# Hash attention and an MLP mixer on one core: a bounce moved into the token stage, a fourth place for its results, and the order of its weight sums

## The chip, the cores and the metric

The kernel runs on one core of a Trainium2 chip. The metric is the device time of one execution in microseconds, and lower is better. TensorE (PE) multiplies matrices into PSUM, VectorE (DVE) and ScalarE (ACT) do elementwise work, GpSimd (POOL) does a little elementwise work and issues the DMAs that add into their destination, and SyncE (SP) issues nearly all other DMAs. Each engine works through its own instructions in program order, and each waits on semaphores of the others.

## The reference

```python
# attention: B=4, H=8, S=768, D=64, hash buckets of 6 bits
q_bits, k_bits = (q @ proj > 0), (k @ proj > 0)
mask = bucket(q_bits)[..., :, None] == bucket(k_bits)[..., None, :]
attn = softmax(where(mask, q @ k.T / sqrt(D), -1e9))
x = (attn @ v).transpose(0, 2, 1, 3).reshape(4, 768, 512)
# mixer: d_tok=256, d_ch=1536, d_model=512
h = relu(x^T @ w_tok1) @ w_tok2
u = x + h^T
out = u + relu(u @ w_ch1) @ w_ch2
```

## The kernel before

Three stages follow each other: `attention`, `tokens`, `channels`. `XT` holds x transposed (features on the partitions) and stays in SBUF all the time. Attention works on 16 pairs of heads, numbered n = 4·batch + pair; 14 of them run in the loop (`NREG` is 14), the last two by a sorted path.

The token stage needs x with rows on the partitions. So each batch is "bounced": `bounce(stage, n)` turns two pairs of `XT` block by block into a staging tile (two DVE transposes, L233) and stores it with four SP DMAs of 192 KB (L238) to a DRAM tile `bounced[b]`; `fetch(b, x)` loads the batch from there (one SP DMA of 1536 KB, L245). Batch 2 is made of bounces 8 and 10, batch 3 of bounce 12 and the sorted pairs. Bounce 10 is `bounce_late`: it runs in the last pair of the attention stage, at the point "newton". Bounce 12 runs at the start of `tokens`.

`tokens` first allocates `x1`, issues `fetch(1, x1)`, starts the conversion of the second channel weight (`Conversion`, three `raw` buffers, 768 KB each by SP at L169; one piece is an ACT pass at L177 and five DVE operations at L187 to L206), and bounces pair 12. Its loop then goes, in program order:

```python
for b in range(B):
    mix1(b)              # PE L1226, x times W1; relu on ACT, L1233; a job per half
    if b == 0:
        weight_sums()    # W2sums, DVE L1203 to L1206
    left_sums(b)         # DVE L1249 to L1252
    if b:
        mix2(b - 1, 0); job(); mix2(b - 1, 1)
mix2(B - 1, 0); inputs(0, T, 0); mix2(B - 1, 1)
```

x of the batches alternates between `x0` and `x1`; `mix1(b)` ends with the fetch of batch b + 2. `mix2(b, m)` is seven products (PE L1266) in four PSUM banks of eight, four ACT copies (L1271 to L1278), five DVE additions (L1281 to L1285), and one POOL DMA of 768 KB that adds the result into `XT` (L1286). The result stands in one of three places, `places[(2b + m + 1) % 3]`, the thirds of `SW2`. The loop has eleven slots for jobs: two in each `mix1`, one between the two `mix2` of each batch but the last. The jobs are the sums of the first channel weight (one job of four DVE operations, L1316 to L1321) and eight pieces of conversion.

`channels` begins with six blocks `hidden(0, t)` of seven products each (PE L1353). In a block ACT copies three products (p1, p5, p7, L1359), DVE adds p1 and a product into `r[0]` (L1393), ACT copies the united product u, and DVE makes `r[3]`, `r[1]`, `r[2]` from it (L1402); POOL adds p5 to p7 (L1397). Sums of weights on DVE (L1858 to L1861, L1316 to L1321) stand between these, one job inside a block and one behind it. In the program order of ACT the copy of u of one block stands ahead of the copy of p1 of the next, and u is copied after the L1393 of its block.

The token stage's own tiles `W1` (6 KB per partition), `W2` (6 KB) and `x0` (12 KB) are laid one behind the other, at 0, 6 and 12 KB from the place where the pool starts. When that pool is closed, the tiles of `channels` are laid over the same bytes in the order of their allocation: `TB` (8 KB) at 0, `R0` (12 KB) at 8, `R1` (12 KB) at 20, and so on. A tile's first writer waits for the last user of the tiles that lay there. `r[0]` of block t is two rows of 1 KB in `R0`, at t KB and at 6 + t KB from its start. The bytes of `x1` belonged to the bit rows and the exponentials (`exps`) of the attention stage, which its last products (PE L470) read.

Of the kernel before, what the change touches and what calls it, by code (L numbers as in the profile page):

```python
# [36 lines left out]
F32 = mybir.dt.float32  # L37
BF16 = mybir.dt.bfloat16
U32 = mybir.dt.uint32
# [9 lines left out]
def kernel(  # L49
# [17 lines left out]
    P = 128  # L67
# [66 lines left out]
    NW = 768  # L134
# [93 lines left out]
    def bounce(stage, n):  # L228

        b, hp = pairs[n]  # L230
        stage = stage.rearrange("p (a k i) -> p a k i", k=2, i=32)
        for k in range(2):
            nc.vector.transpose(  # L233
                stage[:, :, k], XT[:, hp + k, S * b : S * b + S].rearrange("p (a i) -> p a i", i=32),
            )
        to = bounced[b].rearrange("(a i) (g c) -> g i a c", i=32, g=4)
        for g in range(4):
            nc.sync.dma_start(  # L238
                out=to[g, :, :, 32 * hp : 32 * hp + 64],
                in_=stage[32 * g : 32 * g + 32].rearrange("p a k i -> p a (k i)"),  # L240
            )
# [16 lines left out]
    def attention(pool, psum, W1, W2, x0):  # L258
# [725 lines left out]
            at(back + 2, "begin", call("store"))  # L984
        at(0, "loads", prepare_sorting)

        def bounce_late():
            raw = pool.tile([P, NW, 2], U32, name="raw", tag="raw", bufs=2)
            bounce(raw.rearrange("p n w -> p (n w)").bitcast(F32), NREG - 4)

        at(NREG - 1, "newton", bounce_late)
        at(NREG - 1, "begin", fetch_turned)
        at(NREG - 2, "last", lambda: fetch(0, x0))

# [190 lines left out]
    def tokens(pool, psum, W1, W2, x0, weights, jobs, T, places):  # L1185

        x1 = pool.tile([P, NR, DM], F32, name="x1", tag="x1", bufs=1)
        R1 = {}
        turned = not jobs
        if not turned:
            fetch(1, x1)
            jobs = jobs(weights(pool))
            bounce(places[2], NREG - 2)
        NQ = DM // 2
        sums = pool.tile([P, 3, HALF], F32, name="W2sums", tag="W2sums", bufs=1)
        b00, b01, b10, b11 = (W2[:, k, HALF * n : HALF * n + HALF] for k in range(2) for n in range(2))  # L1200

        def weight_sums():
            nc.vector.tensor_tensor(sums[:, 0], b01, b00, op=ALU.subtract)  # L1203
            nc.vector.tensor_tensor(sums[:, 1], b11, sums[:, 0], op=ALU.subtract)
            nc.vector.tensor_tensor(b01, b11, b01, op=ALU.subtract)
            nc.vector.tensor_tensor(sums[:, 2], b10, sums[:, 1], op=ALU.subtract)  # L1206

        def job():
            if not turned and jobs:
                jobs.pop(0)()  # L1210

        def bank(name):
            return psum.tile([P, 512], F32, name=name, tag="mm", bufs=4 if turned else 8)

        def banks():
            return psum.tile([P, 2, 512], F32, name="trp", tag="tr", bufs=2)

        def mix1(b):
            x = (x0, x1)[b % 2]
            if b and turned:  # L1220
                turn(b, x, banks)
            r1 = pool.tile([P, NJ, DM], F32, name="r1", tag="r1", bufs=2)
            for j in range(NJ):
                ps = bank("t1")
                for r in range(NR):
                    nc.tensor.matmul(  # L1226
                        ps, W1[:, r, P * j : P * j + P], x[:, r], start=(r == 0), stop=(r == NR - 1),
                    )
                to = r1[:, j]
                if not turned:  # L1230
                    to = to.rearrange("p (c g i) -> p g c i", c=NCB, i=32)
                    ps = ps.rearrange("p (g c i) -> p g c i", c=NCB, i=32)
                nc.scalar.activation(to, ps, ACT.Relu)  # L1233
                job()
            if b % 2:
                new = pool.tile([P, 3, NQ], F32, name="r1s", tag="r1s", bufs=1)
            else:
                new = T[0].rearrange("p k t -> p (k t)")[:, : 3 * NQ].rearrange("p (i c) -> p i c", i=3)
            R1[b] = r1, new
            if not turned and b + 2 < B:  # L1240
                fetch(b + 2, x)

        def left_sums(b):
            r1, new = R1[b]
            a00, a01, a10, a11 = (
                r1[:, k].rearrange("p (m i c) -> p i m c", m=2, i=2)[:, i] for i in range(2) for k in range(2)
            )
            new = new.rearrange("p i (m c) -> p i m c", m=2)
            nc.vector.tensor_tensor(new[:, 1], a00, a10, op=ALU.subtract)  # L1249
            nc.vector.tensor_tensor(a10, a10, a11, op=ALU.add)  # L1250
            nc.vector.tensor_tensor(new[:, 0], a10, a00, op=ALU.subtract)
            nc.vector.tensor_tensor(new[:, 2], a01, new[:, 0], op=ALU.subtract)  # L1252

        def mix2(b, m):

            r1, new = R1[b]
            a00, a01, s1, a11 = (
                r1[:, k, P * (2 * m + i) : P * (2 * m + i) + P] for i in range(2) for k in range(2)
            )
            new = new[:, :, P * m : P * m + P]  # L1260
            ps = [bank("t2")[:, :HALF] for _ in range(4)]
            to = places[(2 * b + m + 1) % 3].rearrange("p (i n t) -> p i n t", i=2, n=2)
            p1, u, p7, p57 = (to[:, i, n] for i in range(2) for n in range(2))

            def product(at, left, right, start=True):
                nc.tensor.matmul(  # L1266
                    ps[at], left, right, start=start, stop=True, skip_group_check=True,
                )

            product(0, a00, b00)  # L1270
            nc.scalar.copy(p1, ps[0])  # L1271
            product(1, a01, b10)
            product(2, s1, sums[:, 0])
            nc.scalar.copy(p57, ps[2])
            product(3, new[:, 1], b01)
            nc.scalar.copy(p7, ps[3])
            product(0, new[:, 0], sums[:, 1], False)
            nc.scalar.copy(u, ps[0])  # L1278
            product(2, new[:, 2], b11, False)
            product(3, a11, sums[:, 2], False)  # L1280
            nc.vector.tensor_tensor(p1, ps[1], p1, op=ALU.add)  # L1281
            nc.vector.tensor_tensor(p57, p7, p57, op=ALU.add)
            nc.vector.tensor_tensor(p57, p57, u, op=ALU.add)
            nc.vector.tensor_tensor(p7, ps[3], u, op=ALU.add)
            nc.vector.tensor_tensor(u, ps[2], u, op=ALU.add)  # L1285
            nc.gpsimd.dma_start(  # L1286
                out=XT[:, 2 * m : 2 * m + 2, S * b : S * b + S], in_=to.rearrange("p i n t -> p i (n t)"),
                accum_op=ALU.add,
            )

        for b in range(B):
            mix1(b)
            if b == 0:
                weight_sums()
            left_sums(b)
            if b:
                mix2(b - 1, 0)
                job()
                mix2(b - 1, 1)
        mix2(B - 1, 0)  # L1300
        inputs(0, T, 0)
        mix2(B - 1, 1)
        while not turned and jobs:
            job()
# [937 lines left out]
    def attention_and_tokens(W1, W2, x0):  # L2242
        inside(attention, W1, W2, x0)
        pool = late.enter_context(tc.tile_pool(name="late", bufs=1, side="right", reuse_waits="tile"))
        SW1 = big["SW1"] = pool.tile([P, 3, NCB // 2, DCH // 2], F32, name="SW1")
        TA = big["TA"] = pool.tile([P, 2, NCB // 2, TT], F32, name="TA")
        n = NHT * DM

        def second_tile(i):
            return pool.tile([P, (n, n * 3 // 4)[i]], F32, name=f"second{i}", tag=f"second{i}", bufs=1)  # L2250

        WC2 = second["WC2"] = second_tile(0).rearrange("p (k c) -> p k c", k=NHT)
        second["SW2"] = second_tile(1).rearrange("p (i k c) -> p i k c", i=3, k=NHT // 2)
        second["tile"] = second_tile

        def weights(pool):
            return Conversion(pool, [(w_ch2, WC2, 3, (0, NHT))], bufs=3)

        def jobs(conversion):
            early, late = weight_sums(  # L2260
                WC1, SW1, slice(0, NCB // 2), slice(NCB // 2, NCB), slice(0, DCH // 2), slice(DCH // 2, DCH),
            )
            return [
                lambda: (early(), late()),
                *[conversion.one] * (NHT * DM // NW),
            ]

        SW2 = second["SW2"].rearrange("p i k c -> p i (k c)")
        places = [SW2[:, i] for i in range(3)]
        inside(tokens, W1, W2, x0, weights, jobs, [TA[:, 0], None, TA[:, 1], None], places)  # L2270
# [100 lines left out]
```

## Time and profile before

| | |
|---|---|
| median of 3 runs | 766.55 us (766.54 to 766.57) |
| the profiled execution | 767.96 us, span 766.2 us |
| busy in the span | PE 758.5, DVE 673.5, ACT 442.4, POOL 189.7 us |
| the token stage begins (first PE L1226) | 289.1 us |
| the channel stage begins (first PE L1353) | 367.6 us |

Times in the trace are microseconds from the span's start. PE stands for the matmuls and PEld for the weight loads ahead of them; an engine followed by q is its sequencer, so SPq lists the DMAs that SP issues. In a row of the timeline stand start, duration, engine, line, operation, output and inputs, the count, and in square brackets how long the engine had been idle and what ended that.

### The profile page before, as it was taken

What the parts mean: (1) busy time and instruction counts of PE and PEld (TensorE: products, weight loads), DVE (VectorE), ACT (ScalarE), POOL (GpSimd) and SP (SyncE); (2) the same over time, 40 slices, a digit from 0 to 9 for tenths busy, and PEclk for the clock granted to TensorE, in tenths of its full rate; (3) what the DMA queues carried; (4) which work ended last, traced back from release to release, by engine and by line L of the source; (5) the groups of instructions that cost most, each with busy time, mean ns of one, the idle gap of its engine ahead of it and who ended that gap; (6) DMA issues with size and microseconds to landing.
All of it is one profiled execution on the core that took longest, in us unless ns stands there. A gap on an engine that the chain in (4) does not pass through costs nothing.

```text
span 766.2 us, 14575 instructions
## 1 busy us (share of the span) xinstructions
PE 758.5 (99%) x5549; PEld 509.8 (67%) x5549; DVE 673.5 (88%) x969; ACT 442.4 (58%) x816; POOL 189.7 (25%) x266
## 2 busy tenths in 40 slices
PE   9999999999999999999999999999999999999997
PEld 4565655666656554455444468888877888886886
DVE  5899899899997998999788798998899799889884
ACT  6677777677776873333232326566666667665331
POOL 2346771638761820011220100100000011000001
PEclk9999999999999999999999999999999999999999
DMA  7746587575965549876697997889576696750665
GB/s 257 271 172 184 179 240 225 181 179 186 217 202 116 168 68 254 310 178 119 112 321 244 348 360 263 244 233 277 171 220 210 234 261 140 235 157 8 207 157 130
DMA packets 131210, 157.80 MB, mean 206 GB/s; under 512 B 56000, under 2 KB 99520, under 8 KB 129216
## 3 DMA queue, kind: packets, MB, share of 16 engines
q1 hardware_dynamic: 119248, 136.05, 56.3%
q0 software_dynamic: 11600, 20.53, 13.1%
q8 instruction: 45, 0.74, 0.4%
q10 hardware_dynamic: 288, 0.25, 0.1%
q14 instruction: 29, 0.24, 0.1%
HBM read 107.71 MB, written 40.67 MB: 194 GB/s over the span
## 4 chain that ended last, share of the span: by engine, by line
PE 88%; DVE 8%; DMA 2%; issue 1%; SPq 0%; DVEq 0%; ACT 0%; ACTq 0%
PE b L1353 51%; PE sc L503 16%; PE acc L470 14%; PE sc L425 1%; PE hash L536 1%; PE ss L848 1%; DVE size L196 1%; PE sacc L874 1%; DVE unit L195 1%; DMA XT<-second 1%; DVE second L206 1%; PE hash L348 1%; DVE size L191 1%; PE ssums L862 1%; PE hash L353 1%
## 5 line engine op out<-in xcount | busy, mean ns | idle before, releaser
L414 ACT ACTIVATE exps<-sc 128x768 f32<-128x768 f32 (+1 forms) x181 | 126.5, 765 | 10.1 <-PE sc L503 7.2
L1353 PE MATMUL b<-R,second 128*128 128x256 f32 (+1 forms) x522 | 131.8, 408 | 0.0
L503 PE MATMUL sc<-qk 32*128 32x384 f32 (+1 forms) x1352 | 120.1, 457 | 0.0
L1353 PEld LDWEIGHTS b<-R,second 128*128 128x128 f32 x522 | 99.1, 190 | 28.5 <-issue 16.5
L470 PE MATMUL acc<-exps,vn 128*32 128x385 f32 (+1 forms) x1344 | 111.7, 486 | 0.0
L503 PEld LDWEIGHTS sc<-qk 32*128 32x128 f32 x1352 | 92.3, 185 | 16.9 <-issue 4.4
L1359 ACT COPY c<-b 128x256 f32<-128x256 f32 (+1 forms) x96 | 40.3, 426 | 79.3 <-PE b L1353 66.1
L470 PEld LDWEIGHTS acc<-exps,vn 128*32 128x32 f32 x1344 | 43.9, 109 | 62.0 <-issue 60.0
L376 POOL DMA_DIRECT2D bits<-XT x104 | 54.6, 526 | 72.1 <-DVE XT L366 27.4
L459 DVE TENSOR_TENSOR esd<-esd,exps 128x768 f32<-128x768 f32 x70 | 67.0, 957 | 4.3
L1353 PE MATMUL b<-XT,WC 128*128 128x256 f32 (+1 forms) x208 | 61.0, 428 | 0.0
L791 POOL DMA_INDIRECT table<-XT,sorting x48 | 57.1, 1190 | 14.7 <-issue 13.2
L2063 POOL DMA_DIRECT2D out<-second x7 | 8.5, 1213 | 187.3 <-DVE second L2057 81.5
L557 ACT COPY rec<-rec 32x384 f32<-32x384 f32 x56 | 28.5, 510 | 41.0 <-DVE rec L551 39.6
L1353 PEld LDWEIGHTS b<-XT,WC 128*128 128x128 f32 x208 | 39.5, 190 | 15.4 <-issue 10.3
L503 PE MATMUL sc<-bits 32*128 32x384 bf16 (+1 forms) x338 | 48.0, 311 | 0.0
L1353 PE MATMUL b<-XT,SW 128*128 128x256 f32 (+1 forms) x164 | 47.0, 410 | 0.0
L455 DVE TENSOR_TENSOR esd<-esd,exps 128x768 f32<-128x768 f32 x42 | 40.3, 958 | 4.4
L1226 PE MATMUL t<-x,W 128*128 128x512 f32 x96 | 42.1, 594 | 0.2 <-DMA x<-bounced 0.2
L1353 PEld LDWEIGHTS b<-XT,SW 128*128 128x128 f32 x164 | 31.1, 190 | 9.4 <-issue 4.1
L1286 POOL DMA_DIRECT2D XT<-second x8 | 9.9, 1233 | 95.8 <-DVE unit L187 56.2
L1226 PEld LDWEIGHTS t<-x,W 128*128 128x128 f32 x96 | 18.1, 190 | 23.3 <-issue 21.7
(333 smaller groups left out, 1455.9 us busy)
## 6 DMA issues: line engine op xcount, KB each, us to landing
second<-left SPq DMA_DIRECT2D x20, 768.0 KB
qk<-in_qk_rows SPq DMA_DIRECT2D x13, 1152.0 KB
raw<-in_moe_w_ch SPq DMA_DIRECT2D x16, 768.0 KB
second<-left SPq DMA_DIRECT2D x18, 576.0 KB
WC<-hidden_left SPq DMA_DIRECT2D x18, 448.0 KB
x<-bounced SPq DMA_DIRECT2D x4, 1536.0 KB
XT<-second POOLq DMA_DIRECT2D x8, 768.0 KB
seen<-in_qk SPq DMA_DIRECT2D x15, 384.0 KB
```

The source lines that it names most:

```text
L376: nc.gpsimd.dma_start(out=to[at : at + 2 * BITS, half[j]], in_=g[of : of + 2 * BITS])
L414: return nc.scalar.activation(e[:, :, columns], sc, ACT.Exp, scale=SCALE)
L455: nc.vector.tensor_tensor(self.d, self.d, e, op=ALU.add)
L459: nc.vector.tensor_tensor(self.d, self.d, e, op=ALU.add)
L470: made = nc.tensor.matmul(acc[D * i + d : D * i + d + 32], vn[:, i, c, d : d + 32], e[:, i], start=(c == 0), stop=(c == NR - 1),)
L503: nc.tensor.matmul(made[j, piece][:, i], k[at : at + 32, ks], q[at : at + 32], start=part < 0, stop=part == 1,)
L557: nc.scalar.copy(rec[other : other + 32, h], rec[at : at + 32, h])
L791: nc.gpsimd.indirect_dma_start(out=tables[2 * w + i], out_offset=bass.IndirectOffsetOnAxis(ap=self.at[:, x : x + 1], axis=0), in_=row, in_ ...
L1226: nc.tensor.matmul(ps, W1[:, r, P * j : P * j + P], x[:, r], start=(r == 0), stop=(r == NR - 1),)
L1286: nc.gpsimd.dma_start(out=XT[:, 2 * m : 2 * m + 2, S * b : S * b + S], in_=to.rearrange("p i n t -> p i (n t)"), accum_op=ALU.add,)
L1353: nc.tensor.matmul(ps, left(k), right(k), start=start and k == ks[0], stop=stop and k == ks[-1], skip_group_check=True,)
L1359: nc.scalar.copy(c, ps)
```

## The change

Four things: bounce 10 leaves the last pair of attention and is issued at the start of `tokens`, behind the fetch of batch 1 and the first two weight pieces, ahead of bounce 12, through `places[1]`. `weight_sums()` is called ahead of the loop. The last `mix2` writes its result into the first 6 KB per partition of `x0` and not into a third of `SW2`. The sums of the channel weight become two jobs (`early`: L1316, L1317; `late`: L1320, L1321), so that there are ten jobs for the eleven slots.

```diff
-        def bounce_late():
-            raw = pool.tile([P, NW, 2], U32, name="raw", tag="raw", bufs=2)
-            bounce(raw.rearrange("p n w -> p (n w)").bitcast(F32), NREG - 4)
-
-        at(NREG - 1, "newton", bounce_late)
         at(NREG - 1, "begin", fetch_turned)
...
             fetch(1, x1)
             jobs = jobs(weights(pool))
+            bounce(places[1], NREG - 4)
             bounce(places[2], NREG - 2)
...
-            to = places[(2 * b + m + 1) % 3].rearrange("p (i n t) -> p i n t", i=2, n=2)
+            place = places[(2 * b + m + 1) % 3]
+            if b + 1 == B and m:
+                place = x0.rearrange("p r c -> p (r c)")[:, : 2 * S]
+            to = place.rearrange("p (i n t) -> p i n t", i=2, n=2)
...
+        weight_sums()
         for b in range(B):
             mix1(b)
-            if b == 0:
-                weight_sums()
             left_sums(b)
...
-                lambda: (early(), late()),
+                early, late,
                 *[conversion.one] * (NHT * DM // NW),
```

## The prediction

> **What bounds the kernel now.** I read the page first, then the list of waits for PE alone, then the timeline engine by engine around the token stage.
>
> ```profile
> PE 758.5 (99%) x5549; PEld 509.8 (67%) x5549; DVE 673.5 (88%) x969; ACT 442.4 (58%) x816; POOL 189.7 (25%) x266
> PE t L1226 <- DMA x<-bounced: 0.2, 1, 0.2
> ```
>
> PE is busy 758.5 of 766.2 us, and of its listed waits (total, times, longest) this one of 0.2 us is the only one in the token and channel stages. So a removed wait is worth only the hole in PE's matmuls beneath it, and a new wait costs what reaches PE. Matmul ends are modelled, so I measure holes by starts. The chain of waits runs through VectorE from 293 to 358, which I take as a warning about VectorE and not as the bound.
>
> ```profile
> 289.12 10.57 PE L1226 MATMUL t<-x,W 128*128 128x512 f32 x24
> 299.90 10.57 PE L1226 MATMUL t<-x,W 128*128 128x512 f32 x24 [0.22 <-DMA x<-bounced]
> 319.60 10.46 PE L1226 MATMUL t<-x,W 128*128 128x512 f32 x24
> 329.90 1.45 PE L1266 MATMUL t<-W,r 128*128 128x384 f32 x4
> 316.76 0.81 PE L1266 MATMUL t<-W,TA 128*128 128x384 f32 x2
> 317.56 0.30 PEld L1266 LDWEIGHTS t<-W2sums,TA 128*128 128x128 f32 x2 [0.61 <-ACT second L1271]
> 318.31 0.81 PE L1266 MATMUL t<-W,TA 128*128 128x384 f32 x2
> 364.71 0.81 PE L1266 MATMUL t<-W,r1s 128*128 128x384 f32 x2
> 365.07 0.48 ACT L1271 COPY second<-t 128x384 f32<-128x384 f32 x1 [2.91 <-DMA XT<-second]
> 366.35 0.81 PE L1266 MATMUL t<-W,r1s 128*128 128x384 f32 x2
> 367.64 3.60 PE L1353 MATMUL b<-XT,WC 128*128 128x512 f32 x8
> ```
>
> An unhindered `mix1` takes 329.90 - 319.60 = 10.30 us. The first took 299.90 - 289.12 = 10.78, because batch 1 had not landed: a hole of 0.48. Four undisturbed matmuls of `mix2` take 367.64 - 366.35 = 1.29. From 316.76 to 318.31 they took 1.55 (hole 0.26), and from 364.71 to 366.35 they took 1.64 (hole 0.35). The last hole is the copy at 365.07, which waited for a place. All that the change can win here is 0.48 + 0.26 + 0.35 = 1.09 us, 0.14%. A difference of 0.2%, 1.53 us, is about what a measurement of this kernel tells from none.
>
> **The change part by part. Attention's end.**
>
> ```profile
> 285.03 2.15 ACT L557 COPY rec<-rec 32x384 f32<-32x384 f32 x4 [3.71 <-DVE rec L551]
> 285.51 1.83 DVE L233 STREAM_TRANSPOSE raw<-XT 128x768 f32<-128x768 f32 x2
> 287.26 0.92 DVE L561 TENSOR_TENSOR XT<-num,rec 128x768 f32<-128x768 f32 x1
> 285.13 4.06 PE L470 MATMUL acc<-exps,vn 128*32 128x384 f32 x48
> 287.37 3.11 SPq L238 DMA_DIRECT2D bounced<-raw  x4
> 290.65 1.12 SPq L245 DMA_DIRECT2D x<-bounced  x1
> ```
>
> The two transposes of bounce 10 leave a hole in VectorE: the next instruction, L561, needs ACT's copies, which end at 287.18. Removing them wins nothing there (0 to 0.1). On SP the four stores go from ahead of the fetch of batch 1. That fetch then waits for the exponentials under `x1`, which PE reads until 285.13 + 4.06 = 289.2, so it goes 1.45 us earlier. It took 299.90 - 290.65 = 9.25 to be of use, so it would be there by 298.4, ahead of PE at 289.12 + 10.30 = 299.4: the hole of 0.48 closes (0 if the load gains nothing).
>
> **The token stage on SP.**
>
> ```profile
> 297.57 6.35 SPq L238 DMA_DIRECT2D bounced<-second  x4
> ```
>
> Four stores took SP 6.35 us beside the loads. Now eight stand in a row, behind the transposes that still begin at 295.70 (below): at worst to 297.57 + 12.7 = 310.3. Behind them on SP wait the fetch of batch 2 and the third weight piece. A fetch of 9.25 lands at 319.5, PE wants it at 319.60 less 0.48 and 0.26: between 0 and 0.7 us of wait, and I take 0, since the first weight pieces now load earlier. Nor does it matter, as the next step shows. `places[1]` is first rewritten by ACT around 311, after those stores.
>
> **The token stage on DVE.**
>
> ```profile
> 295.70 1.84 DVE L233 STREAM_TRANSPOSE second<-XT 128x768 f32<-128x768 f32 x2
> 304.48 0.56 DVE L187 TENSOR_SCALAR unit<-size 128x768 uint32<-128x768 uint32 x1
> 308.47 0.55 DVE L1203 TENSOR_TENSOR W2sums<-W 128x384 f32<-128x384 f32 x1
> 357.60 0.56 DVE L1285 TENSOR_TENSOR second<-t,second 128x384 f32<-128x384 f32 x1
> 361.55 0.56 DVE L1282 TENSOR_TENSOR second<-second 128x384 f32<-128x384 f32 x1 [0.28 <-ACT second L1276]
> 357.94 1.16 PEld L1266 LDWEIGHTS t<-W,r 128*128 128x128 f32 x4
> 359.87 0.51 PEld L1266 LDWEIGHTS t<-W,r1s 128*128 128x128 f32 x2
> ```
>
> From 295.70 on the timeline marks no idle VectorE until 361.55. So 1.84 us of added transposes shift what follows. The split job moves each conversion piece (308.47 - 304.48 = 3.99) one slot later, so between the first `left_sums` and the last conversions VectorE is 3.99 - 1.84 = 2.15 us early. That makes the first six `mix2` safe, and removes the copy's delay at 317 (0.26 won; 0 if the third weight piece lands late). But the eighth piece then fills the slot of the last `mix1` that was empty, and from `left_sums(3)` on VectorE is 1.84 late. The L1285 of `mix2(2, 0)` ends at 358.16 + 1.84 = 360.0. `mix2(3, 0)` takes over that call's PSUM banks: its weight loads came at 357.94 to 359.87, and would now come 0.48 + 0.26 = 0.74 earlier, but its fourth product needs the bank that L1285 frees. PE is there at 360.06 instead of 359.87: what was won is given back, whatever it was. Cost against before 0.2, bounds -0.74 (bank not needed) to 0.2. The fourth place then removes the wait at 365.07: -0.35. `weight_sums` ahead of the loop is needed later than before and costs nothing of its own. PE enters `channels` about 0.2 us earlier.
>
> **The fourth place.** The place is `x0`'s first 6 KB, bytes 12 to 18 KB of the pool. `R0` lies at 8 to 20 KB, and `r[0]` of block 0 writes 8 to 9 and 14 to 15 KB. So its L1393 must wait until the last accumulating DMA has read the place.
>
> ```profile
> 374.71 1.07 ACT L1359 COPY c<-b 128x512 f32<-128x512 f32 x2 [2.79 <-PE b L1353]
> 358.57 1.20 POOL L1286 DMA_DIRECT2D XT<-second  x1 [6.89 <-DVE second L1285]
> 365.30 1.22 POOL L1286 DMA_DIRECT2D XT<-second  x1 [5.53 <-issue]
> 372.05 1.20 POOL L1286 DMA_DIRECT2D XT<-second  x1 [5.53 <-DVE TB L1183]
> 378.80 1.21 POOL L1286 DMA_DIRECT2D XT<-second  x1 [5.55 <-DVE seen L1859]
> 376.48 0.69 DVE L1393 TENSOR_TENSOR R<-b,c 128x512 f32<-128x512 f32 x1 [5.29 <-ACT c L1359]
> 377.21 0.59 ACT L1359 COPY c<-b 128x512 f32<-128x512 f32 x1 [1.43 <-DVE R L1393]
> 386.52 1.88 PE L1353 MATMUL b<-TB,SW 128*128 128x512 f32 x4
> ```
>
> The last four of these DMAs follow each other on POOL by 6.73 to 6.75 us. The first was read out 365.07 - 358.57 = 6.50 after its start (that ended ACT's wait for the place). With L1285 1.84 later, the last starts at 378.80 + 1.84 = 380.64 and is done at 387.14; without the shift at 385.30. L1393 ran at 376.48: a new wait of some 10.7 us on VectorE. Behind L1393 on VectorE wait the block's other sums and the weight sums; ACT's copy of u waits for L1393 (377.21), and behind it in ACT's order stands the next block's p1, without which PE can't overwrite that bank. So: L1393 at 387.15, u at 387.9, p1 at 388.4 to 389.0 (a copy takes 0.59, two in a row 1.07), PE at 389.05 instead of 386.52. PE loses 2.5 us against before. POOL's own queue is 1.84 later, and nothing there is wanted before VectorE comes free.
>
> ```profile
> 302.80 1.76 DVE L1321 TENSOR_TENSOR SW<-WC,SW 128x1536 f32<-128x1536 f32 x1
> 379.20 2.53 DVE L1861 TENSOR_TENSOR seen<-SW,seen 128x384 f32<-128x384 f32 x1
> 389.41 2.71 DVE L1321 TENSOR_TENSOR second<-second,second 128x1536 f32<-128x1536 f32 x1
> 392.04 0.68 DVE L1393 TENSOR_TENSOR R<-b,c 128x512 f32<-128x512 f32 x1
> 398.54 1.88 PE L1353 MATMUL b<-TB,SW 128*128 128x512 f32 x4
> ```
>
> The next L1393 stands 392.04 - 376.48 = 15.56 us of VectorE work later. Two of its instructions were stretched beside POOL's additions: L1861 by 1.97 (2.53 against the 0.56 of an addition of that size, as L1285 above), L1321 by 0.95 (2.71 against 1.76 at 302.80). The first meeting falls away, since VectorE is waiting then. So it comes at 387.15 + 15.56 - 1.97 = 400.7 (399.8 with neither, 402.7 with both), the second block's p1 is ready 1.8 later as above, and PE goes on at 402.55 instead of 398.54: 4.0 lost in all. From there VectorE is 8.7 late and PE 4.0. The banks of a block are wanted only two blocks on, and a p1 copy that is late by the difference still stands ahead of its PE instruction, so I add nothing.
>
> The sum: 4.0 us on PE's path, which from 367.64 to the end has no hole to take it up. The profiled execution, 767.96, stands 1.4 above the median; the difference is added to the median: 766.55 + 4.0 = 770.5.
>
> **The Trainium skill** ("DMA: Bandwidth & Descriptors", section "Anatomy of one DMA — SWDGE (gpsimd) path") fits a DMA issued from GpSimd as about 2.0 us plus its bytes at 436e3 per us, an estimate of 3.8 us for 768 KB. By that the last one would end at 360.4 + 4 x 3.8 = 375.6, ahead of L1393, and the sum would be 766.3. These rows disagree: 6.75 between starts, 6.50 to the end.
>
> **The rivals.** *A: the accumulate lands in time.* It decides at about 382.8: then L1393 is soon enough for both p1 copies. If the last one started when its sums are ready, at some 370, and took 6.50, it would be done at 376.6. Then 766.55 less 0.2 to 1.09, so 765.5 to 766.3, not slower. Against it stand three equal steps of 6.75 on POOL. The skill's fit would lead here too. *B: the wait is real and PE feels half.* VectorE not later at 358, reading done at 385.30, PE late 0.7 and then 1.3 to 2.2: 767.8 to 768.7. *C: it doesn't end there.* VectorE 8.7 late runs into the stores of its one scratch tile, and at the second layer's first sums it is still late: with both meetings and another stall of 2 us, 772.6 to 774.
>
> **How the numbers follow.** Forecast (3.1 to 6.0 lost, that is 769.6 to 772.6) 0.64; B 0.17; C 0.07; A 0.12. The range 767.8 to 772.6 takes in the forecast and B. Slower by over 0.2% needs over 1.53 us: forecast, C, and most of B, 0.86. Within 0.2%: most of A and the edge of B, 0.11. Faster by over 0.2% needs more than the 1.09 that the holes hold: 0.03.
>
> **What would show it.** In the new trace L1393 of the first block is idle some 10 us, ended by the DMA into XT; PE's list of waits gains the ACT copies of L1359 in the second and third block, 2.5 and 1.5 us; four L1286 still stand 6.75 apart, the last near 380.6; the hole at 299 is gone; `mix2(3, 0)` waits for VectorE. I am wrong if the last L1286 starts before 376, or if L1393 stays near 376.5.

## The result

The changed kernel took 771.07 us (median of 4 runs, 770.79 to 771.38), before 766.55: a ratio of 1.0059, 95% interval 1.0042 to 1.0076. It is slower, by 4.5 us where 4.0 were forecast (770.5).

The profiled execution, 770.79 with a span of 769.1 us, shows where. First its list of waits for PE (total, times, longest):

```profile
PE b L1351 <- ACT c L1357: 3.4, 2, 2.0
PE t L1222 <- DVE second L1280: 0.5, 1, 0.5
PE t L1265 <- ACT second L1270: 0.4, 1, 0.4
PE b L1351 <- DVE R L2004: 0.2, 1, 0.2
```

Lines have moved by a few: L1226 is now L1222, L1266 L1265, L1271 L1270, L1281 L1280, L1286 L1285, L1321 L1319, L1353 L1351, L1359 L1357, L1393 L1391, L1397 L1395, L1402 L1400. Before, one wait of 0.2 us stood for both stages; now the first row holds two waits, in the second and third block of `channels`. The attention stage of this execution ended 1.67 us earlier than in the one of before, so I compare times from the first `mix1` on. PE in the timeline:

```profile
287.45 20.87 PE L1222 MATMUL t<-x,W 128*128 128x512 f32 x48
315.81 0.91 PE L1265 MATMUL t<-W2sums,TA 128*128 128x384 f32 x2 [0.40 <-ACT second L1270]
318.53 10.57 PE L1222 MATMUL t<-x,W 128*128 128x512 f32 x24 [0.52 <-DVE second L1280]
366.33 3.60 PE L1351 MATMUL b<-XT,WC 128*128 128x512 f32 x8
383.50 1.88 PE L1351 MATMUL b<-TA,SW 128*128 128x512 f32 x4
387.38 1.98 PE L1351 MATMUL b<-TB,SW 128*128 128x512 f32 x4 [2.01 <-ACT c L1357]
397.79 1.88 PE L1351 MATMUL b<-TA,SW 128*128 128x512 f32 x4
401.09 1.98 PE L1351 MATMUL b<-TB,SW 128*128 128x512 f32 x4 [1.42 <-ACT c L1357]
```

The first row holds both `mix1` of batches 0 and 1 without a break: the hole at 299 is gone. Two new holes stand at 315.81 and 318.53. The token stage took 366.33 - 287.45 = 78.88, against 367.64 - 289.12 = 78.52 before: +0.36. The rest of the span took 402.77 against 398.56: +4.21. Four such matmuls take 1.72 undisturbed. From 383.50 to 387.38 and from 397.79 to 401.09 they took 3.88 and 3.30; with 0.1 in the matmul behind each, PE lost about 2.27 and 1.69 there, and by the same measure 0.48 at 459. VectorE and POOL show the cause:

```profile
358.71 1.20 POOL L1285 DMA_DIRECT2D XT<-second  x1 [10.84 <-DVE second L1284]
378.96 1.21 POOL L1285 DMA_DIRECT2D XT<-x  x1 [5.55 <-PE b L1351]
385.53 0.69 DVE L1391 TENSOR_TENSOR R<-b,c 128x512 f32<-128x512 f32 x1 [14.62 <-DMA XT<-x]
386.26 2.05 ACT L1357 COPY c<-b 128x512 f32<-128x512 f32 x4 [11.79 <-DVE R L1391]
388.39 1.54 POOL L1395 TENSOR_TENSOR c<-c 128x512 f32<-128x512 f32 x1 [6.92 <-ACT c L1357]
388.72 1.76 DVE L1400 TENSOR_TENSOR R<-c 128x512 f32<-128x512 f32 x1
397.57 1.76 DVE L1319 TENSOR_TENSOR second<-second,second 128x1536 f32<-128x1536 f32 x1
399.24 0.68 DVE L1391 TENSOR_TENSOR R<-b,c 128x512 f32<-128x512 f32 x1
```

The first block's sum waited 14.62 us, until the last accumulating DMA, started at 378.96, had read the fourth place: 6.57 later. The copies on ACT waited for it (11.79), and PE for the copies. L1319 is not stretched now (1.76). POOL's addition of p5 and p7 falls beside the first L1400 instead, which reads its result and takes 1.76, where the same sum took 0.68 before (L1402 at 381.65). The next L1391 follows 13.71 after the first.

### The profile page after: what moved, and what is told of

It reads as the page before. It is cut to its first block, busy times and chain, and to the rows that moved or that the text cites. A ratio compares the mean times of both kernels' runs of the same rounds, so it can differ in the third digit from the quotient of the medians.

```text
span 769.1 us, 14578 instructions
## 1 busy us (share of the span) xinstructions
PE 756.7 (98%) x5549; PEld 505.6 (66%) x5549; DVE 671.9 (87%) x969; ACT 442.5 (58%) x816; POOL 191.1 (25%) x266
## 4 chain that ended last, share of the span: by engine, by line
PE 82%; DVE 9%; issue 4%; DMA 2%; ACT 1%; POOL 1%; DVEq 0%; POOLq 0%; SPq 0%; ACTq 0%
PE b L1351 45%; PE sc L503 14%; PE acc L470 12%; PE t L1222 3%; PE t L1265 2%; PE hash L536 1%; PE sc L425 1%; PE ss L848 1%; PE sacc L874 1%; DMA hidden_left<-second 1%; DMA XT<-x 1%; PE ssums L862 1%; PE hash L348 1%; ACT exps L414 1%; POOL bits L376 1%
## 5 line engine op out<-in xcount | busy, mean ns | idle before, releaser
L1351 PE MATMUL b<-R,second 128*128 128x256 f32 (+1 forms) x522 | 132.0, 409 | 0.2 <-DVE R L2004 0.2
L1351 PEld LDWEIGHTS b<-R,second 128*128 128x128 f32 x522 | 99.0, 190 | 29.0 <-issue 17.1
L503 PEld LDWEIGHTS sc<-qk 32*128 32x128 f32 x1352 | 90.5, 185 | 19.7 <-issue 5.9
L1357 ACT COPY c<-b 128x256 f32<-128x256 f32 (+1 forms) x96 | 39.9, 427 | 77.1 <-PE b L1351 49.3
L791 POOL DMA_INDIRECT table<-XT,sorting x48 | 58.8, 1224 | 15.2 <-issue 13.8
L1351 PE MATMUL b<-XT,WC 128*128 128x256 f32 (+1 forms) x208 | 61.0, 428 | 0.0
L1351 PEld LDWEIGHTS b<-XT,WC 128*128 128x128 f32 x208 | 39.5, 190 | 15.4 <-issue 11.0
L1351 PE MATMUL b<-XT,SW 128*128 128x256 f32 (+1 forms) x164 | 47.0, 410 | 0.0
L1222 PE MATMUL t<-x,W 128*128 128x512 f32 x96 | 41.9, 594 | 0.5 <-DVE second L1280 0.5
L1351 PEld LDWEIGHTS b<-XT,SW 128*128 128x128 f32 x164 | 31.1, 190 | 9.4 <-issue 4.7
L1222 PEld LDWEIGHTS t<-x,W 128*128 128x128 f32 x96 | 18.1, 190 | 23.6 <-issue 22.2
L1285 POOL DMA_DIRECT2D XT<-second x7 | 8.7, 1237 | 92.1 <-DVE unit L187 54.1
```

Source lines behind the costliest of these rows:

```text
L503: nc.tensor.matmul(made[j, piece][:, i], k[at : at + 32, ks], q[at : at + 32], start=part < 0, stop=part == 1,)
L791: nc.gpsimd.indirect_dma_start(out=tables[2 * w + i], out_offset=bass.IndirectOffsetOnAxis(ap=self.at[:, x : x + 1], axis=0), in_=row, in_ ...
L1222: nc.tensor.matmul(ps, W1[:, r, P * j : P * j + P], x[:, r], start=(r == 0), stop=(r == NR - 1),)
L1351: nc.tensor.matmul(ps, left(k), right(k), start=start and k == ks[0], stop=stop and k == ks[-1], skip_group_check=True,)
L1357: nc.scalar.copy(c, ps)
```

## The experiments

The attention stage's length varied from one execution to the next (the first `mix1` began between 287.45 and 290.71), so beside each ratio I give the lengths from the trace: the token stage (first `mix1` to first block of `channels`; before 78.52) and everything from the first `mix1` to the end of the span (before 477.08, changed 481.65).

| run | ratio to before (95%) | token stage | first `mix1` to the end |
|---|---|---|---|
| e1: changed, without the fourth place | 1.0020 (1.0010 to 1.0031) | 80.32 | 478.62 |
| e2: before, with the fourth place alone | 1.0037 (1.0023 to 1.0050) | 78.16 | 480.15 |
| e3: changed, place given to the sixth `mix2` | 1.0009 (0.9998 to 1.0020) | 78.87 | 477.27 |
| e4: changed, DMAs as plain copies | 1.0012 (1.0000 to 1.0023) | 78.87 | 477.18 |
| e5: before, place for the sixth `mix2` | 1.0006 (0.9996 to 1.0015) | 78.18 | 476.56 |
| e6: changed, upper half of `x0` | 1.0069 (1.0054 to 1.0085) | 78.88 | 481.83 |
| e7: e3, third weight piece first | 1.0000 (0.9991 to 1.0009) | 78.88 | 477.29 |
| e9: e5 and the order of the sums | 0.9990 (0.9979 to 1.0001) | 77.77 | 476.37 |
| e10: e9, four stores on POOL | 1.0000 (0.9991 to 1.0009) | 78.46 | 477.32 |
| e11: e10, third weight piece first | 0.9987 (0.9978 to 0.9996) | 77.46 | 476.23 |
| e13: changed, without four sums | 1.0061 (1.0047 to 1.0074) | 78.87 | 481.49 |
| e14: e2, without four sums | 1.0068 (1.0055 to 1.0082) | 78.16 | 479.91 |

**Is it the place or the rest of the change?**

```diff
 # e1 (from the changed kernel)
-            if b + 1 == B and m:
-                place = x0.rearrange("p r c -> p (r c)")[:, : 2 * S]
 # e2 (from the kernel before)
+            if b + 1 == B and m:
+                place = x0.rearrange("p r c -> p (r c)")[:, : 2 * S]
```

> The changed kernel with the last mix2 back in a third of SW2; everything else of the change stays. Theory (the fourth place under R0 costs the 4.2 us in the channel stage, and the later VectorE work is a smaller price of its own): no wait of the first block's sum for a DMA, no stall of PE in the second and third block; but the copy of the last mix2 again waits for the fifth accumulating DMA, which starts 1.8 later than before (started 358.71 + 6.5 = 365.2 in the changed kernel's clock, wanted at 362.66), so PE loses about 1.5 there: 766.55 + 0.36 + 1.5 = 768.4, range 767.3 to 768.8. Rival (the moved bounce and the order of VectorE are at fault, the place is not): 771, with the stalls in the second and third block still there.

> The kernel before with the fourth place for the last mix2 and nothing else. Theory (the place is enough for the wait; VectorE's 1.8 only sets how long it is): the hole of 0.35 at the last mix2 goes; the last accumulating DMA starts at 378.8, so the first block's sum runs at 385.4 instead of 376.5; PE loses 1.05 in the second block and 1.7 in the third: 766.55 - 0.35 + 1.05 + 1.7 = 768.95, with the small later stall 769.4; range 768.4 to 769.8. Rival (the wait hurts only together with the moved bounce): 766.2 to 766.9.

e1 measured 768.55, 1.44 over its runs of before (767.11). The stalls in `channels` are gone, and the copy waits for its place as expected, 1.46 lost at 366:

```profile
365.73 0.48 ACT L1268 COPY second<-t 128x384 f32<-128x384 f32 x1 [4.01 <-DMA XT<-second]
377.14 0.69 DVE L1389 TENSOR_TENSOR R<-b,c 128x512 f32<-128x512 f32 x1 [5.35 <-ACT c L1355]
```

So the moved bounce has a price of its own, which the fourth place hides in the changed kernel: VectorE's results are 1.8 later, and with three places the last copy is later by nearly as much. e2 measured 770.05, 2.94 over before: a little over the range given (the scale of those runs was 0.6 higher; the difference expected was 2.4 to 2.85).

```profile
377.82 1.21 POOL L1289 DMA_DIRECT2D XT<-x  x1 [5.55 <-issue]
384.38 0.69 DVE L1396 TENSOR_TENSOR R<-b,c 128x512 f32<-128x512 f32 x1 [13.92 <-DMA XT<-x]
457.52 0.95 DVE L2009 TENSOR_TENSOR R<-R,c 128x768 f32<-128x768 f32 x1
```

The place alone brings the wait (6.56 from POOL's start to L1396), and PE lost 1.14, 1.69 and, at L2009, 0.69. The place is what costs. In the changed kernel the last DMA starts 1.84 later than here, counted from the first `mix1`, and PE enters `channels` 0.72 later, so its first stall is longer by 1.1.

**Which wait is it: the bytes, the tile, the length of the DMA?**

```diff
 # e3 (from the changed kernel)
-            if b + 1 == B and m:
-                place = x0.rearrange("p r c -> p (r c)")[:, : 2 * S]
+            if not turned and 2 * b + m >= 5:
+                place = (x0.rearrange("p r c -> p (r c)")[:, : 2 * S], places[1], places[0])[2 * b + m - 5]
 # e4 (from the changed kernel)
-                accum_op=ALU.add,
 # e6 (from the changed kernel)
-                place = x0.rearrange("p r c -> p (r c)")[:, : 2 * S]
+                place = x0.rearrange("p r c -> p (r c)")[:, 2 * S :]
```

> The changed kernel with the place in x0 given to the sixth mix2 (second half of batch 2) instead of the eighth; the seventh writes to places[1], the eighth to places[0]. The DMA out of x0 then starts near 365.4 and is done near 372, ahead of the first block's sum at 375. Theory: no wait for a place anywhere, no stall in the channels; what is left of the change is its token stage, 0.36 longer than before: 766.9, range 766.4 to 767.3. Rival (R0 waits for something else than this DMA, or any result under R0 costs): 769 to 771.

> The changed kernel with the eight DMAs from POOL into XT as plain copies: the addition of x is left out, the same bytes are moved. Theory (adding is what makes 6.5 us of each): a plain copy of 768 KB lands in some 3.3 to 4 us, POOL's starts are spaced by the sums and not by 6.75, the last one starts near 371 to 373 and is done by 377; the first block's sum waits 2 us or less, PE does not stall: 766.9, range 766.3 to 767.5. Rival (the 6.75 is POOL's or the queue's time for such a DMA, whatever it does): starts still 6.7 apart, 771.

> The changed kernel with the last mix2's result in the upper 6 KB of x0 and not in the lower. Those bytes lie under the last 2 KB of R0 and the first 4 KB of R1, and no r[0] of the first four blocks touches them. My prediction argued with bytes: then the first block's sum (L1391) would run at 375 and the wait move to r[1] (the second of L1400, some 378 to 385). Rival (waits go by whole tiles: R0 overlaps x0, so its first writer waits for x0's last reader): L1391 still waits to some 385.5, the same stalls of 2.3 and 1.7, and 771.

e3 took 0.43 over before, and no stall is left in `channels`: with the same tile lent out two DMAs earlier, L1391 is released by PE.

```profile
366.43 1.22 POOL L1285 DMA_DIRECT2D XT<-x  x1 [5.55 <-ACT second L1275]
376.14 0.69 DVE L1391 TENSOR_TENSOR R<-b,c 128x512 f32<-128x512 f32 x1 [4.51 <-PE b L1351]
```

e4, with the addition of x left out, took 0.79 over before. The DMAs of POOL:

```profile
359.78 0.71 POOL L1285 DMA_DIRECT2D XT<-second  x1 [11.51 <-DVE second L1284]
362.67 0.71 POOL L1285 DMA_DIRECT2D XT<-second  x1 [2.18 <-ACT second L1277]
365.07 0.72 POOL L1285 DMA_DIRECT2D XT<-second  x1 [1.69 <-DVE second L1284]
370.24 0.71 POOL L1285 DMA_DIRECT2D XT<-x  x1 [4.45 <-issue]
376.23 0.69 DVE L1390 TENSOR_TENSOR R<-b,c 128x512 f32<-128x512 f32 x1 [4.26 <-PE b L1350]
```

Copies of the same 768 KB start 2.89 and 2.40 apart; adding ones start 6.75 apart. So the 6.75 belongs to adding into the destination, and not to POOL or its queue. The last copy is done before 376.23 and nobody waits.

e6 falsifies a step of mine. No `r[0]` of the first four blocks touches the upper half of `x0`, and yet:

```profile
386.44 0.69 DVE L1391 TENSOR_TENSOR R<-b,c 128x512 f32<-128x512 f32 x1 [14.73 <-DMA XT<-x]
```

The same wait, the same stalls, 5.0 us over before. The first write to `R0` waits for the last reader of what lies under the whole of `R0`, whichever bytes it writes itself. The upper half of `x0` does lie under the last 2 KB of `R0`, so e6 doesn't show whether reading bytes outside `R0` would make it wait too. Neither half of `x0` is harmless here.

**The token stage: two holes, one cause.** In the changed kernel the third weight piece landed at 314.4 (SP fetches it behind batch 2, since the first conversion is a job later), which held up ACT's copies; and the first matmul of `mix1(2)` waited for L1280, VectorE's first sum of `mix2(0, 0)`. Before, it waited for no such sum: `mix1(2)` began at 319.60, and the same sum ran later.

```profile
321.73 0.55 DVE L1281 TENSOR_TENSOR second<-t,second 128x384 f32<-128x384 f32 x1
```

So `mix1(2)` begins in another PSUM bank than before: in one that VectorE frees. The banks are dealt out when the program is built. What changed the deal isn't shown.

```diff
 # e7 (from e3)
-            jobs = jobs(weights(pool))
+            conversion = weights(pool)
+            conversion.fetch()
+            jobs = jobs(conversion)
             bounce(places[1], NREG - 4)
```

> The changed kernel with the sixth mix2 in x0, and the third weight piece fetched right behind the first two, ahead of both bounces. In the changed kernel and its three variants so far, the hole ahead of the second mix2 of batch 0 (third piece late) and the one ahead of the first mix1 of batch 2 (PSUM bank freed by VectorE) measured 0.66 + 0.79, 1.00 + 0.43, 1.25 + 0.19, 0.75 + 0.70: the sum is the same. Theory (VectorE's sum that frees the bank sets the end, the late piece only takes a part of the same wait): the first hole is gone, the second becomes 1.35 to 1.45, and the time is that of the variant without this edit, 0.4 over before (766.9 to 767.1). Rival (the late piece costs its own 0.66 to 1.25): the second hole stays at 0.2 to 0.8, and the time falls by 0.6 or more.

```profile
290.71 20.87 PE L1224 MATMUL t<-x,W 128*128 128x512 f32 x48
321.79 4.56 PE L1224 MATMUL t<-x,W 128*128 128x512 f32 x10 [1.19 <-DVE second L1282]
369.59 2.74 PE L1353 MATMUL b<-XT,WC 128*128 128x512 f32 x6
```

The first hole is gone, the second is 1.46, and the token stage is 78.88 as without the edit. `mix1(2)` begins 31.08 after the first `mix1` here, and 318.53 - 287.45 = 31.08 in the changed kernel: VectorE sets it, and the late piece hid inside that wait. e11 below is dealt the other bank: there `mix1(2)` begins 29.73 after the first, ahead of VectorE's sum (319.39). And e9 below is e3 without the moved bounce: its sum begins 28.76 after the first `mix1` and not 30.47, and its token stage is 77.77 and not 78.87. So the moved bounce costs 1.1 us of the token stage, although it closes the hole at 299.

**A version that keeps the gains.**

```diff
 # e5 (from the kernel before): the place as in e3
 # e9 (from e5)
+        weight_sums()
         for b in range(B):
             mix1(b)
-            if b == 0:
-                weight_sums()
...
-                lambda: (early(), late()),
+                early, late,
 # e10 (from e9): the four stores of bounce 10 issued by POOL, transposes stay in attention
-    def bounce(stage, n):
+    def bounce(stage, n, queue=nc.sync):
...
-            nc.sync.dma_start(
+            queue.dma_start(
...
-            bounce(raw.rearrange("p n w -> p (n w)").bitcast(F32), NREG - 4)
+            bounce(raw.rearrange("p n w -> p (n w)").bitcast(F32), NREG - 4, nc.gpsimd)
 # e11 (from e10): conversion.fetch() as in e7
```

> The kernel before with only the place in x0 given to the sixth mix2, the seventh to places[1], the eighth to places[0]. Theory (a place under R0 is free of cost when its DMA is done before the first block's sum): the copy of the last mix2 waits no longer, its hole of 0.35 goes, nothing comes in its place: 766.2, that is 0.35 under before, range 766.0 to 766.5. Rival (any place in x0 costs): 768 or more.

> The kernel before with the sixth mix2 in x0, the weight sums ahead of the loop and the channel weight's sums as two jobs; bounce 10 stays in the last pair of attention. Theory: the hole of 0.35 goes with the place, and the one of 0.26 at the second mix2 of batch 0 goes because VectorE's conversions come a slot later: 766.55 - 0.61 = 765.95, range 765.6 to 766.4. Rival (the split alone makes VectorE free the bank of mix1 of batch 2 too late, or the third piece late): 766.5 to 767.2, with a hole there.

> As the one with place and order, and the four stores of bounce 10 are issued by POOL, which is idle from 275 to 324, in place of SP. Theory (what held the fetch of batch 1 back was SP's queue, not VectorE's transposes): the fetch starts 1.4 earlier, the hole of 0.48 at 299 goes, without 1.84 of VectorE moved into the token stage: 766.55 - 0.35 - 0.26 - 0.48 = 765.45, range 765.1 to 766.1. Rival (four stores by POOL land so late that batch 2 is late, or they slow down the fetch): 766 to 768 with a wait of mix1 of batch 2 for its load.

> As the one with bounce 10's stores on POOL, and the third weight piece fetched right behind the first two. In that run the hole of 0.48 at 299 was gone, but the third weight piece, behind batch 2's fetch, which waited for POOL's last store till 306.2, was late by 1.03 at the second mix2 of batch 0. Theory: that hole goes, no other comes: token stage 77.4 where before has 78.5, 766.55 - 1.1 = 765.45, range 764.9 to 766.2. Rival (VectorE sets the end again, or batch 2 is late): token stage 78 or more, 766.2 to 767.

e5 (767.79 against 767.70) cannot be told from before by its times; its token stage is 0.34 shorter, as expected. e9 took 766.95 (0.75 less); its token stage is 0.75 shorter, and no hole is left at 317. e10 closed the hole at 299 and opened another: POOL issued its four stores over 16 us where SP takes 3.1, batch 2's fetch waited for them on SP, and the third weight piece was late behind it (1.03 at the second `mix2`).

```profile
287.01 0.80 POOL L238 DMA_DIRECT2D bounced<-raw  x1 [13.59 <-DVE raw L233]
303.01 0.73 POOL L238 DMA_DIRECT2D bounced<-raw  x1 [5.11 <-issue]
316.91 0.91 PE L1269 MATMUL t<-W2sums,TA 128*128 128x384 f32 x2 [0.76 <-ACT second L1274]
```

e11 takes that away with the third piece first: 766.56 against 767.60 on its chip, ratio 0.9987 (0.9978 to 0.9996), the only run here whose interval lies below one. Its token stage is 77.46, 1.06 less than before, which is nearly all of the 1.09 that the holes held:

```profile
288.87 20.87 PE L1228 MATMUL t<-x,W 128*128 128x512 f32 x48
318.60 7.89 PE L1228 MATMUL t<-x,W 128*128 128x512 f32 x18
319.39 0.55 DVE L1286 TENSOR_TENSOR second<-t,second 128x384 f32<-128x384 f32 x1
366.33 3.60 PE L1357 MATMUL b<-XT,WC 128*128 128x512 f32 x8
```

**The later stalls.** Are they VectorE's backlog?

```diff
 # e13 (from the changed kernel), e14 (from e2)
-                [hidden_parts("p7")], sums, [whole("p1"), second_parts("p7")], *([second_parts(name)] for name in ("p6", "p3", "p5", "p2", "p4")),
+                [hidden_parts("p7")], [], [whole("p1"), second_parts("p7")], *([second_parts(name)] for name in ("p6", "p3", "p5", "p2", "p4")),
```

> The changed kernel without the four sums of the second channel weight on VectorE behind the first block (L1314 to L1319, 7.04 us; what would use them reads old data). Theory (the second stall is VectorE's backlog: the wait's delay plus this work): the first stall of 2.28 stays, the second of 1.69 goes, the later one of 0.48 goes: 771.07 - 2.2 = 768.9, range 768.4 to 769.4. Rival (the second stall comes from the copies or the DMAs): 770.5 to 771.1.

> The kernel before with the fourth place alone, and without the four sums of the second channel weight on VectorE behind the first block (what would use them reads old data). In the run of the changed kernel without these sums the second stall was gone, but behind the first hole of 2.68 us (start to start) stood a stretch of 3.4 us with the granted clock at 0.50, which cost 1.66. Here the first hole is 1.3 to 1.5. Theory (the second and third stalls are VectorE's backlog; the clock falls only behind the longer hole): first stall 1.14 as with the place alone, no others, no stretch at half clock: 2.37 less than with the place alone, which was 2.94 over before, so 0.6 over before, range 0.1 to 1.2 over. Rival 1 (the second stall comes from the copies or DMAs): 2.5 to 3 over. Rival 2 (a stretch at half clock follows the shorter hole too, when no second stall takes it up): 2.2 over.

Both missed in time: 772.22, 4.6 over before, and 771.84, 4.8 over. The second stall did go in both, so it came from VectorE's work behind the wait. But the gain came back in another place each time. In e14 (PE):

```profile
PE b L1356 <- DVE R L2009: 1.9, 1, 1.9
PE b L1356 <- ACT c L1362: 0.8, 1, 0.8
```

PE lost 1.11 in the second block and then 2.15 at the second layer's first sums, in place of 0.69. VectorE had 7 us less to do, but it now waits for its scratch tile (`seen`), whose stores stand on SP behind the stores of the first block's sums and of the residual. VectorE and SP in e14:

```profile
388.99 0.34 SPq L1880 DMA_DIRECT2D hidden_left<-seen  x1
392.40 3.72 SPq L2137 DMA_DIRECT2D out<-XT  x4
397.53 1.43 SPq L1872 DMA_DIRECT2D left<-seen  x1
404.95 0.56 DVE L1861 TENSOR_TENSOR seen<-second 128x384 f32<-128x384 f32 x1 [6.95 <-DMA left<-seen]
449.67 0.96 DVE L1950 TENSOR_TENSOR second<-R 128x768 f32<-128x768 f32 x1 [1.20 <-DMA hidden_left<-second]
```

The last of these is the first instruction that prepares the second layer. It and the first store, in the kernel before and then in the changed one:

```profile
381.75 0.34 SPq L1877 DMA_DIRECT2D hidden_left<-seen  x1
445.77 0.96 DVE L1947 TENSOR_TENSOR second<-R 128x768 f32<-128x768 f32 x1 [0.53 <-DMA hidden_left<-second]
```

```profile
388.83 0.34 SPq L1875 DMA_DIRECT2D hidden_left<-seen  x1
449.54 0.96 DVE L1945 TENSOR_TENSOR second<-R 128x768 f32<-128x768 f32 x1 [0.75 <-DMA hidden_left<-second]
```

The preparing instruction is released by a store each time. Counted from the first `mix1`, the first store starts 8.75 later than before in the changed kernel and 6.87 in e14; the instruction is late by 5.44 in the changed kernel, 3.78 in e2, 3.53 in e14 and 4.78 in e13; the end is late by 4.57, 3.07, 2.83 and 4.41.

So two paths lead from the one wait to the end: PE's own stalls, and SP's row of stores, which starts when the delayed scratch sums are ready. Whichever is later sets the time. In e14 the chain that ended last runs through VectorE and these stores, without PE, from the first block's sum at 385.69 to L2009. In the changed kernel it runs through PE from 401.09 to 439.14, and only then through a last store, which holds L1945 until 449.54. In e13 PE had lost another 1.7 on the way by its clock (last section), so the stores did not stop it again. That explains the profiled executions only. Two other executions of e13 list a mean clock of 1.00 and still took 772.46 and 772.71. What they lost, and what the other four runs of e14 (771.7 to 774.1, its profiled one 771.08) lost beyond this, stays open.

## Why the prediction was right, and where it was wrong

- **Fourth place, the wait.** Right: L1391 was expected at 387.15 and ran at 385.53, which is 387.20 on the clock of before (+1.67). The accumulate took 6.57 from its start (6.50 assumed). Right for a partly wrong reason: the argument from bytes 14 to 15 KB isn't what makes the wait (e6); the whole of `R0` does.
- **First stall.** Right: PE was expected to go on at 389.05, and did at 387.38, which is 389.05 on the clock of before. That is 2.53 late against before (2.5 forecast), of which 0.36 came from the token stage. Since the copies say when PE goes on, an earlier PE would only have waited longer: the mistake in the token stage (below) cost nothing here.
- **Second stall.** 402.55 forecast; 401.09 measured, 402.76 on the clock of before, 4.2 late where 4.0 was forecast. VectorE's next L1391 came 13.71 after the first (13.59 forecast), and that is partly luck. The forecast kept the 0.95 by which L1321 had been stretched beside POOL. L1319 was not stretched, but L1400 was longer by 1.08 beside POOL, whose result it reads (whether the meeting or the result held it isn't shown); without that it would have been 12.63.
- **"Nothing later".** Wrong by 0.48: at 459 PE waited for L2004. This is rival C's mechanism, the one scratch tile and its stores, at a smaller price than C gave. It isn't a remainder of the second stall: in e14, where that is gone, it is 2.15.
- **Token stage.** The step that failed. Forecast: 0.15 gained, with a wait of `mix2(3, 0)` for VectorE that gives back 0.74. Measured: 0.36 lost. The hole of 0.48 did close and the wait of 0.35 for a place went. But the third weight piece, which I let cost only the hoped-for 0.26, landed at 314.4 and cost 0.66 in its place; and `mix1(2)` met a PSUM bank that VectorE freed late, 0.79, of which nothing stood in the prediction. VectorE was early there, as forecast (L1280 ran 30.48 after the first `mix1`, before 32.61). What failed is the conclusion that this makes the first six `mix2` safe: it took for granted that PE goes on in the same bank. PE so came 0.7 later to `mix2(3, 0)`, and did not wait there for VectorE.
- **Sum.** 4.0 forecast, 4.52 by the medians, 4.57 by the traces. PE's last long group of matmuls starts 4.80 later than before, counted from the first `mix1`: 0.36 in the token stage, and 2.27 + 1.69 + 0.48 in `channels`. The last store starts 4.80 later too, and the span ends 4.20 behind it and not 4.43.
- **Rivals.** A fell because the accumulates do stand 6.7 apart. With the addition left out (e4) the stalls go, as A needs, but the time is not below before, as A had it: 0.79 over by the runs, 0.10 by the traces, with a token stage 0.35 longer. The Trainium skill's fit ("DMA: Bandwidth & Descriptors", "Anatomy of one DMA — SWDGE (gpsimd) path"), 3.8 us by an estimate, disagrees with the adding DMAs; the copies of e4 start 2.4 to 2.9 apart, and their landing isn't shown. B's case is e2: PE is 0.68 late at the second block (0.7 in B) and 2.36 at the third (1.3 to 2.2); with the later stall the whole of e2, 2.94, lies above B's range.

## What to carry to other kernels

Before lending a dead tile as a buffer, ask when its last reader is done and which tile is laid over it next: with waits by tile, any overlap makes the next owner's first write wait for that reader. The same loan two steps earlier cost nothing here (e3, e5). Work moved to a busy engine (1.84 us on VectorE) can be paid wherever that engine frees something, a PSUM bank here; and if a late buffer starts a queue of stores, taking away the engine's own work behind it doesn't bring the time back.

## What the runs showed of the hardware

Accumulating SBUF-to-SBUF DMAs of 768 KB from POOL started 6.7 to 6.8 us apart in a row; as plain copies (e4) two started 2.40 apart. Four stores of 192 KB from POOL started over 16 us (287.01 to 303.01, e10), where SP took 3.1 for the same four before.

Behind the first stall of e13, PE ran at half its clock. Windows of e13 (columns: length, busy time and count of PE, PEld, DVE, ACT, POOL, then the granted clock, DMA share, GB/s):

```profile
389.40:389.80 0.40, 0.40 (x2) 0.21 (x1) 0.40 (x1) 0.40 (x2) 0.00 (x0) 0.63 0.00 0
390.60:391.40 0.80, 0.80 (x3) 0.28 (x2) 0.80 (x1) 0.00 (x0) 0.80 (x1) 0.50 0.22 92
392.60:393.00 0.40, 0.40 (x2) 0.04 (x1) 0.40 (x2) 0.17 (x1) 0.00 (x0) 0.61 0.94 369
```

The time at 0.50, with its share of the two windows at the ends, is 0.30 + 2.80 + 0.31 = 3.41 us (the windows between read 0.50), and PE lost about 1.7. The Trainium skill ("TensorE: Matmul & The Clock Gate", "Part 1: The HAM clock gate (the "warmup" mystery)") gives a free-running window of 3413 ns and half the clock after an idle one. The trace agrees on the length and the ratio. It doesn't agree on what it takes: the hole here was 2.68 from start to start, shorter than a window, and holes of 2.60 in the changed kernel and 2.70 in e6 were followed by a clock of 1.00. Whether the window's phase decides isn't shown. The three other executions of the changed kernel list mean clocks of 0.997 and 0.998 and took 0.2 to 0.6 us longer than the profiled one at 1.000; whether they had such a stretch isn't shown.
